# A recurrent attention block and a gated product: seven products for eight in the last six half blocks, with chunks placed every two steps and reordered sums

## The chip, the cores and the metric

The kernel runs on one core of a Trainium2 chip. Its engines work side by side, each through its own queue in order, and wait for each other by semaphores: PE multiplies matrices, DVE and POOL do elementwise work, ACT does activations and copies, SP issues most of the DMAs. Matmuls read SBUF and add up in PSUM[...]. The metric is the device time of one execution in microseconds (us), and the median over several runs is compared.

## The reference

All numbers are float32 on the chip (the two weight matrices of the second half come as float64 and are converted by the kernel).

```python
batch, n_heads, seq, head_dim = (4, 8, 768, 64)
gamma = 1.0 - 2.0 ** (-5.0 - np.arange(H))
for t in range(S):
    state = gamma[None, :, None, None] * state + np.einsum('bhd,bhe->bhde', k[:, :, t], v[:, :, t])
    y[:, :, t] = scale * np.einsum('bhd,bhde->bhe', q[:, :, t], state)

x = y.transpose(0, 2, 1, 3).reshape(B * S, H * D)      # 3072 x 512
h = x @ w_in                                           # 3072 x 2048
g = h - np.tanh(h)
out = g @ w_out                                        # 3072 x 512
```

## The kernel before

**Two halves that overlap.** The attention works in 24 chunks of 128 tokens (six to a batch). The second half works on 12 *half blocks* of 256 tokens (n = 0 to 11; a chunk is half of one), and within each on 8 tiles of 256 of the 2048 middle columns (m2 = 0 to 7). That makes 96 steps. The list `steps` (L492) has half blocks 0 to 3 first, in pieces of two or four tiles while the weights still arrive (32 steps), then half blocks 4 to 11 one after the other, eight tiles each (64 steps).

**One step** is an up product (`up`, L407: 8 matmuls of 256 columns into a bank h), an activation, and a down product (`down`, L456) of the tile two steps back (`LAG = 2`): for each of the two token halves j, two matmuls of 512 columns that add into a bank of output. The trace shows each float32 matmul of the program as two passes, so an up product has 16 passes and a down product 8.

**The activation** has five ACT instructions (`shrink_begin` L420, `shrink_factors` L427: a square, a tanh, two more squares and a relu), three DVE instructions (`shrink_multiply`, L436) and three more (`shrink_end`, L445), which leave g. The last tile of a run of tiles is followed by `add_up` (L465), which copies or adds the output bank into `sum` on DVE or ACT, and starts the store of the output on SP when the last weights are in it.

**A chunk of attention** is spread over three chunk steps. `load_chunk` (L222) loads k, q, v. `scale` (L232, on POOL) multiplies q and v by a power of gamma. `turn_by_dma` (L267) brings k and q into transposed form: two ACT copies split the words into 16-bit halves (`apart`, L273), SP stores them to DRAM (`rows`, L276) and reads them back through a transposing DMA into `kqT` (L278). `products` (L287) multiplies k with v (L298) and `kqT` with itself (L304, the scores); `mask` and `state` take the results off PSUM on DVE; `outputs` and `outputs_rest` (L336, L385) multiply into y (L352) with `see` (small ACT copies) between them; `keep_x` (L389) copies y into `xT`, the input of the up products.

**The order** is the program's own: nothing is moved by a scheduler. The first eight chunks and steps follow an order written out by hand (L547). From step 8 on the loop at L569 runs. `with_chunk` (L564) gives every third step a chunk ci: the step scales chunk ci+3, ends the outputs of ci, makes the products of ci+2, loads ci+4 and begins the outputs of ci+1. Its last act is to turn chunk ci+3. Steps 9 to 26 also convert one piece of weights each (four DVE instructions and two each on ACT and POOL) and load another on SP.

```python
with_chunk = {BEGUN + 3 * i + 1: FIRST - 3 + i for i in range(NCH - FIRST + 3)}
...
for s in range(BEGUN, len(steps)):
    ...
    shrink_begin(n, m2)
    shrink_factors(n, m2)
    shrink_multiply(n, m2)
    shrink_end(n, m2)
    downs(LAG)
    if ci is not None and ci + 3 < NCH:
        turn_by_dma(ci + 3)
```

PSUM is full: two banks for k and q products ("t"), two for y, two for h and two for the output sums ("o").

## The time and the profile before

| what | value |
|---|---|
| median of 9 runs | 754.64 us (754.43 to 755.52) |
| the profiled execution | 754.64 us, of which the span of the instructions is 752.8 us |
| granted clock of PE | 1.00 of full speed throughout |
| busy in 100 to 200 us: PE, DVE, ACT, POOL | 99.1, 91.6, 65.3, 48.6 us |
| busy in 350 to 450 us | 100.0, 61.4, 51.4, 8.2 us |
| busy in 550 to 650 us | 100.0, 59.9, 43.2, 0 us |
| DVE operation on 128x512, on 128x256 | 0.69 us, 0.42 us |
| POOL operation on 128x512 | 1.09 to 1.29 us |
| store of 256 KB of output, issue to landing | 2.0 us |

The span is the time from the first to the last instruction of one execution that the hardware profiler recorded. The three stretches are one with attention and weights still arriving, one with attention alone, and one with neither. An engine's queue is in order, so a wait of one instruction delays all behind it on that engine; but idle time of an engine that isn't the one that sets the end costs nothing.

### The profile page before, as it was taken

The page shows a single profiled execution, that of the slowest core. Times are in us where ns is not written, and L with a number is a line of the kernel's source. Part 1 is how long each engine was busy: PE and PEld are TensorE (multiplying, and loading weights), DVE is VectorE, ACT ScalarE, POOL GpSimd, SP SyncE. Part 2 cuts the span into 40 slices and gives each one's busy share as a digit, 9 for nine tenths or more (in the row PEclk, how much of TensorE's full clock was granted, in tenths as well). Part 3 has the DMA queues.
Part 4 walks back from the last instruction along what each step waited for, and adds up shares of the span by engine and source line. Part 5 has one row for each costly group of instructions (what it writes and reads, how often), then busy time and mean ns, then how long its engine had stood idle before and what let it go on. Part 6 is the DMA issues. An engine that isn't in the chain of part 4 may idle for free.

```text
span 752.8 us, 13801 instructions
## 1 busy us (share of the span) xinstructions
PE 740.1 (98%) x5470; PEld 502.4 (67%) x5470; DVE 519.4 (69%) x807; ACT 389.1 (52%) x725; POOL 126.6 (17%) x108
## 2 busy tenths in 40 slices
PE   8799999999999999999999999999999999999997
PEld 7686666666667676766676666666666666666663
DVE  4999889998898666656565656555665666556653
ACT  4567486667665545445545545444344434433441
POOL 0564445435453111100111100000000000000000
PEclk9999999999999999999999999999999999999999
DMA  9882436556553353332542412000000000000000
GB/s 204 210 213 59 127 99 179 148 151 157 151 128 90 92 137 118 85 85 76 107 99 73 97 57 58 28 1 1 29 0 1 28 1 0 29 0 1 28 2 28
DMA packets 125392, 59.76 MB, mean 79 GB/s; under 512 B 109840, under 2 KB 118160, under 8 KB 125328
## 3 DMA queue, kind: packets, MB, share of 16 engines
q1 hardware_dynamic: 125184, 58.73, 30.3%
q8 instruction: 43, 0.70, 0.4%
q10 hardware_dynamic: 144, 0.15, 0.1%
q14 instruction: 21, 0.17, 0.1%
HBM read 35.80 MB, written 14.68 MB: 67 GB/s over the span
## 4 chain that ended last, share of the span: by engine, by line
PE 87%; DVE 7%; DMA 2%; ACT 1%; issue 1%; SPq 1%; POOL 0%; DVEq 0%; ACTq 0%; POOLq 0%
PE h L414 40%; PE o L462 40%; PE y L352 3%; PE s L298 1%; PE s L304 1%; DVE head L185 1%; DMA raws<-in_moe_w_in_dram 1%; DVE h L448 1%; DVE g L452 1%; DVE head L183 1%; DVE h L442 1%; DMA q<-in_q_dram 1%; DMA k<-in_k_dram 1%; DVE th L439 1%; DVE g L453 1%
## 5 line engine op out<-in xcount | busy, mean ns | idle before, releaser
L414 PE MATMUL h<-xT,w 128*128 128x256 f32 x1536 | 349.9, 381 | 1.1 <-DVE w L199 1.1
L462 PE MATMUL o<-w,g 128*128 128x512 f32 x768 | 345.6, 593 | 1.4 <-DVE sum L471 0.9
L414 PEld LDWEIGHTS h<-xT,w 128*128 128x128 f32 x1536 | 289.7, 190 | 71.8 <-issue 34.0
L462 PEld LDWEIGHTS o<-w,g 128*128 128x128 f32 x768 | 145.4, 190 | 145.7 <-issue 136.6
L423 ACT ACTIVATE u<-h 128x512 f32<-128x512 f32 x96 | 57.4, 598 | 292.0 <-PE h L414 292.0
L439 DVE TENSOR_TENSOR th<-h,th 128x512 f32<-128x512 f32 x96 | 66.2, 690 | 176.0 <-ACT th L424 175.8
L453 DVE COPY_PREDICATED g<-large,th 128x512 f32<-128x512 int32 x96 | 72.2, 752 | 10.6 <-ACT apart L273 0.5
L442 DVE SCALAR_TENSOR_TENSOR h<-q,h 128x512 f32<-128x512 f32 x96 | 66.8, 696 | 10.4 <-DVE h L440 0.5
L448 DVE SCALAR_TENSOR_TENSOR h<-q,h 128x512 f32<-128x512 f32 x96 | 66.8, 696 | 9.9
L431 ACT ACTIVATE q<-u,tab 128x512 f32<-128x512 f32 x96 | 69.4, 723 | 0.0
L432 ACT ACTIVATE q<-u,tab 128x512 f32<-128x512 f32 x96 | 69.0, 719 | 0.0
L433 ACT ACTIVATE large<-u,tab 128x512 f32<-128x512 f32 x96 | 68.7, 716 | 0.0
L452 DVE TENSOR_TENSOR g<-h,u 128x512 f32<-128x512 f32 x96 | 66.3, 691 | 3.3
L440 DVE SCALAR_TENSOR_TENSOR h<-u,h 128x512 f32<-128x512 f32 x96 | 65.8, 685 | 0.0
L236 POOL TENSOR_TENSOR q<-q,tab 128x512 f32<-128x512 f32 x22 | 24.1, 1093 | 199.4 <-DMA q<-in_q_dram 158.1
L424 ACT ACTIVATE th<-h 128x512 f32<-128x512 f32 x96 | 56.8, 591 | 0.0
L195 POOL TENSOR_TENSOR low<-low,power 128x512 f32<-128x512 f32 x30 | 38.7, 1289 | 102.3 <-DVE power L187 78.1
L199 POOL TENSOR_TENSOR w<-low,head 128x512 f32<-128x512 f32 x30 | 38.5, 1282 | 2.4
L352 PEld LDWEIGHTS y<-a,v 64*64 64x64 f32 x768 | 15.8, 134 | 16.2 <-ACT large L433 10.6
L236 POOL TENSOR_TENSOR v<-v,tab 128x512 f32<-128x512 f32 x22 | 26.5, 1204 | 0.0
L382 ACT COPY seen<-y 64x1 f32<-64x1 f32 x96 | 10.1, 153 | 24.7 <-PE y L352 24.3
L393 ACT COPY xT<-y 128x512 f32<-128x512 f32 x24 | 14.1, 587 | 16.4 <-PE y L352 16.4
(49 smaller groups left out, 382.9 us busy)
## 6 DMA issues: line engine op xcount, KB each, us to landing
rows<-apart SPq DMA_DIRECT2D x16, 512.0 KB, 2.6
k<-in_k_dram SPq DMA_DIRECT2D x24, 256.0 KB, 4.0
q<-in_q_dram SPq DMA_DIRECT2D x24, 256.0 KB, 4.9
v<-in_v_dram SPq DMA_DIRECT2D x24, 256.0 KB, 5.3
raw<-in_moe_w_out_dram SPq DMA_DIRECT2D x12, 512.0 KB, 3.5
out_dram<-sum SPq DMA_DIRECT2D x24, 256.0 KB, 2.0
raw<-in_moe_w_in_dram SPq DMA_DIRECT2D x14, 256.0 KB, 4.1
raw<-in_moe_w_in_dram SPq DMA_DIRECT2D x28, 128.0 KB, 3.8
```

The lines of the kernel that those rows point to most:

```text
L414: nc.tensor.matmul(hp, w1[:, c, ts(2 * m2 + i, P)], xT[n // 2][:, c, ts(n % 2, TH)], start=(i == 0 and c == 0), stop=(c == NC - 1), skip_g ...
L423: nc.scalar.activation(u, hp, AF.Square)
L431: nc.scalar.activation(q0, u, AF.Square, bias=bias0)
L432: nc.scalar.activation(q1, u, AF.Square, bias=bias1, scale=math.sqrt(A))
L433: nc.scalar.activation(large, u, AF.Relu, bias=bias_m)
L439: nc.vector.tensor_tensor(th, hp, th, op=ALU.subtract)
L440: nc.vector.scalar_tensor_tensor(hp, in0=u, scalar=R, in1=hp, op0=ALU.subtract, op1=ALU.mult, reverse0=True)
L442: nc.vector.scalar_tensor_tensor(hp, in0=q0, scalar=C0, in1=hp, op0=ALU.add, op1=ALU.mult)
L448: nc.vector.scalar_tensor_tensor(hp, in0=q1, scalar=A * C1, in1=hp, op0=ALU.add, op1=ALU.mult)
L452: nc.vector.tensor_tensor(flat, hp, u, op=ALU.mult)
L453: nc.vector.copy_predicated(flat, large.bitcast(I32), th)
L462: nc.tensor.matmul(o_p[j], gT[n, m2][:, i, ts(j, P)], w2[:, 2 * m2 + i], start=(first and i == 0), stop=(last and i == 1))
```

## The change

The last six half blocks (n = 6 to 11) compute the down product by Winograd's form of Strassen's scheme. The 256 tokens are split into two sets of 128, the 256 middle columns into two of 128, and the 512 output columns into two of 256. Eight products of blocks become seven, with sums of blocks before and after:

- `fast_sums` makes four sums of blocks of g on POOL, 128x128 each, in each of the 48 steps.
- `fast_weights` makes four differences of blocks of the weights for each pair of tiles, 16 operations on POOL in all, one in each of the steps 33 to 48, in buffers that the weights' conversion and one `xT` no longer need.
- `fast_down` issues the seven matmuls, 256 columns wide, into halves of the banks that the attention and the sums held.
- `fast_end` recombines the seven results once for a half block: one ACT copy, seven DVE operations of 256 columns and two stores.

So that those banks are free, the chunks come every two steps rather than three and are over after step 45 (before: step 63). The outputs of the last chunk come behind the up product of their step. `downs` comes ahead of `shrink_end`. The tokens of a half block are dealt out alternately to its two sets, which makes `keep_x` two copies and the rows of each output store alternate.

```diff
@@ keep_x
-        nc.scalar.copy(
-            out=xT[n][:, :, ts(nj, P)].rearrange("p (n r) t -> p r n t", r=2),
-            in_=y_banks[:, ci % 2][:, :: 1 - 2 * (ci % 2)],
-        )
+        half = xT[n][:, :, ts(nj // 2, TH)].rearrange("p (n r) t -> p r n t", r=2)
+        y = y_banks[:, ci % 2][:, :: 1 - 2 * (ci % 2)]
+        for odd in range(2):
+            nc.scalar.copy(out=half[:, :, :, ds(P * odd + D * (nj % 2), D)],
+                           in_=y[:, :, :, odd::2])
@@ add_up
-            nc.sync.dma_start(out=out[ds(n * TH + j * P, P)], in_=o)
+            nc.sync.dma_start(out=rows_of(n)[:, j], in_=o)
...
+    FAST = 6
+    PAIRS = NM // 2
+    def quarter(i, c, at):
+        return w2[:, i::2, ts(c, TH)][:, ds(2 * at, 2)]
+    def fast_weights(k, at):
...
+        t = t_of[k, at] = room[PAIRS // 2 * k + at]
+        a, b = (
+            (quarter(0, 1, at), quarter(0, 0, at)),
+            (quarter(1, 1, at), t_of.get((0, at))),
+            (quarter(1, 1, at), quarter(0, 1, at)),
+            (t_of.get((1, at)), quarter(1, 0, at)),
+        )[k]
+        nc.gpsimd.tensor_tensor(t, a, b, op=ALU.subtract)
+    def fast_sums(n, m2):
+        g = gT[n, m2]
+        a11, a12, a21, a22 = (g[:, i, ts(j, P)] for j in range(2) for i in range(2))
+        s_ = inp.tile([P, 4, P], F32, tag="kq"[m2 % 2], name=f"s_{n}_{m2}", bufs=2)
+        s1, s2, s3, s4 = (s_[:, i] for i in range(4))
+        nc.gpsimd.tensor_tensor(s1, a21, a22, op=ALU.add)
+        nc.gpsimd.tensor_tensor(s2, s1, a11, op=ALU.subtract)
+        nc.gpsimd.tensor_tensor(s3, a11, a21, op=ALU.subtract)
+        nc.gpsimd.tensor_tensor(s4, a12, s2, op=ALU.subtract)
+        fast_g[n, m2] = (a11, a12, s4, a22, s1, s2, s3)
...
+    def fast_down(n, m2, first, last):
+        if first:
+            fast_banks(n)
+        left = fast_g.pop((n, m2))
+        for k in (1, 6, 5, 7, 4, 2, 3):
+            right = (
+                w2[:, 2 * m2, :TH], w2[:, 2 * m2 + 1, :TH], w2[:, 2 * m2 + 1, TH:],
+                *(t_of[x, m2 // 2][:, m2 % 2] for x in (3, 0, 1, 2)),
+            )[k - 1]
+            nc.tensor.matmul(accs[n][k], left[k - 1], right, start=first and k in (1, 6, 5, 4),
+                             stop=last, skip_group_check=True)
+    def fast_end(n):
+        acc = accs.pop(n)
+        o = op.tile([P, 2, DM], F32, tag="sum", name=f"sum_{n}")
+        c11, c12, c21, c22 = (o[:, j, ts(c, TH)] for j in range(2) for c in range(2))
+        some = [mid.tile([P, 2, TH], F32, tag="a", name=f"fast_{n}") for _ in range(2)]
+        p1, v_, x_, w_ = (t[:, i] for t in some for i in range(2))
+        nc.scalar.copy(out=p1, in_=acc[1])
+        for dst, k, b, how in (
+            (v_, 6, p1, add), (x_, 5, v_, add), (w_, 7, v_, add), (c22, 5, w_, add),
+            (c21, 4, w_, sub), (c11, 2, p1, add), (c12, 3, x_, add),
+        ):
...
@@ downs
+            if tile_[0] >= FAST:
+                fast_down(*tile_)
+                if tile_[3]:
+                    fast_end(tile_[0])
+                continue
@@ the loop
-    with_chunk = {BEGUN + 3 * i + 1: FIRST - 3 + i for i in range(NCH - FIRST + 3)}
+    with_chunk = {BEGUN + 2 * i + 1: FIRST - 3 + i for i in range(NCH - FIRST + 3)}
+    with_fast = {4 * NM // 2 + 1 + i: (i % 4, i // 4) for i in range(2 * PAIRS)}
...
-            if FIRST <= ci + 1 < NCH:
+            if FIRST <= ci + 1 < NCH - 1:
                 outputs(ci + 1)
                 see(ci + 1)
...
         for i in range(2):
             up(n, m2, i)
+        if ci == NCH - 2:
+            outputs(ci + 1)
+            see(ci + 1)
         waiting.append(steps[s])
         shrink_begin(n, m2)
         shrink_factors(n, m2)
         shrink_multiply(n, m2)
+        downs(LAG)
         shrink_end(n, m2)
-        downs(LAG)
+        if n >= FAST:
+            fast_sums(n, m2)
+        if s in with_fast:
+            fast_weights(*with_fast[s])
         if ci is not None and ci + 3 < NCH:
             turn_by_dma(ci + 3)
-    for j in range(2):
-        for tile_ in waiting:
-            part(j, *tile_)
+    downs(0)
```

The lines move by some numbers: what is L298 and L304 before is L302 and L308 after, `up` is L420, the new matmuls are L579.

## The prediction

> **What bounds the kernel now.** I read the busy times first, then the chain of waits, the chain's pieces late in the run, one whole chunk period on three engines, the DMA issues and the tail.

> ```profile
> span 752.8 us, 13801 instructions
> ...
> PE 740.1 (98%) x5470; PEld 502.4 (67%) x5470; DVE 519.4 (69%) x807; ACT 389.1 (52%) x725; POOL 126.6 (17%) x108
> ...
> PE 87%; DVE 7%; DMA 2%; ACT 1%; issue 1%; SPq 1%; POOL 0%; DVEq 0%; ACTq 0%; POOLq 0%
> ...
> 596.87 3.45 PE h L414 x16
> 600.33 3.43 PE o L462 x8
> ```

> PE works almost always and carries the chain: what leaves PE's queue shortens the run, what makes PE wait lengthens it. The last two lines are one step: an up product of 16 passes of 256 columns (3.45/16 = 0.2155 us each) and a down product of 8 passes of 512 columns (3.43/8 = 0.429). A step is 6.89 us.

> The second thing to read is one chunk period (timeline of PE, ACT and SP, times from the span's start).

> ```profile
> 330.74 0.46 PE L352 MATMUL y<-a,v 64*64 64x64 f32 x16
> 331.02 0.65 PE L298 MATMUL s<-v,k 64*64 64x64 f32 x32
> 331.49 0.65 PE L304 MATMUL s<-kqT 64*64 64x64 f32 x32
> 332.77 3.72 PE L414 MATMUL h<-xT,w 128*128 128x256 f32 x16
> 336.53 0.60 ACT L423 ACTIVATE u<-h 128x512 f32<-128x512 f32 x1 [3.17 <-PE h L414]
> 339.34 1.04 ACT L273 COPY apart<-k 128x1024 uint16<-128x1024 uint16 x1
> 340.27 1.05 ACT L273 COPY apart<-q 128x1024 uint16<-128x1024 uint16 x1
> 341.34 0.36 SPq L276 DMA_DIRECT2D rows<-apart  x1
> 344.03 1.86 SPq L278 DMA_TRANSPOSE kqT<-rows  x1
> 353.63 0.46 PE L352 MATMUL y<-a,v 64*64 64x64 f32 x16
> 354.38 0.65 PE L304 MATMUL s<-kqT 64*64 64x64 f32 x32
> ...
> kqT<-rows SPq DMA_TRANSPOSE x16, 4.2
> ```

> Call 330.74 the chunk's start. The transposed k and q of the next chunk come out of a fixed chain: up product, five activations, two copies to `apart` (over at +10.6), a store of `rows` that lands 2.7 later, and a transposing DMA that lands 4.1 to 4.2 after its issue, at +17.4. L304 of the next chunk needs them. It comes at 354.38, +23.6, so the chain has 6.2 us to spare and PE never shows a wait on it.

> The tail:

> ```profile
> 743.71 5.42 PE L462 MATMUL o<-w,g 128*128 128x512 f32 x12 [0.51 <-DVE g L453]
> 749.17 0.69 DVE L473 COPY sum<-o 128x512 f32<-128x512 f32 x1 [5.51 <-PE o L462]
> ```

> [...] the transpose is issued 2.69 us after `rows`, as soon as that has landed (2.6). Two such DMAs in series can't be pipelined within a chunk. [...] Here a load takes 190 ns against 215 ns of a 256-column pass, so halving the width stays just clear of the load. [...]

> **The change part by part.**

> *Seven products for eight.* For half blocks 6 to 11 (48 of 96 steps) a down product of 8 passes of 512 becomes 7 products of 256 columns, two passes each: 14 x 0.2155 = 3.02 us for 3.43. The loads have the up product's shape, which keeps 0.2155. Gain 0.42 x 48 = 20.2 us. If each pass lost 5 ns to loads it would be 16.8; below 0.2155 nothing points.

> *POOL's sums.* Four 128x128 operations per step stand between g and the product. POOL's 512-wide ones take 1.09 to 1.29; [...] a quarter of a row's time is 0.32, a full row's 1.29 bounds it. I take 0.4, 1.6 for four. A g is ready 5.6 us after its up product (600.33 to 605.94), its down product starts 12.9 after, so 7.3 is spare; with 2.9 of recombination before `shrink_end`, 4.4. Hidden, even nearly at the upper bound; only the last step shows it, about 0.2. The 16 weight differences (1.2 to 1.3 each, steps 33 to 48) lie in POOL's idle time.

> *Recombination.* Seven DVE operations of 256 columns (0.42, from the `state` rows) and an ACT copy per half block, before `shrink_end`. DVE has 40% idle there (59.86 busy of 100 in 550 to 650). Hidden five times, exposed once: the program lets the first of the seven wait for the last product of the bank it reads, so for the last half block all seven (3.05 us) follow the last matmul, against 0.69 now. From the end of the last up product (738.07) the span now lasts 14.7. After: three down products 9.05, stalls 0.3, 3.05, and 2.94 for the store as now, 15.3. So the end is 0.6 worse though three of the 48 savings (1.26) fall into it: 1.9 is taken off the 20.2.

> *Sums ahead of the last operations.* DVE's sums come out before L448. It removes the 0.86 us wait of PE for a sum at 144.5, and puts stores of out ahead of `rows` on SP. g gets 1.2 later where 7 are spare.

> *Last chunk's outputs behind an up product.* Removes a 0.70 us wait of PE for `xT` at 491.9.

> *x in two column halves.* Two ACT copies of 256 for one of 512: 0.2 longer, 24 times, beside ACT idle of 1 to 3 us before each square. I take 0.2 for the crowded opening, bounds 0 and 1.

> *Chunks every two steps instead of three.* `3 * i` becomes `2 * i`, so the attention's banks are free after step 45. The chunk period now is 353.63 - 330.74 = 22.89; with one step of 6.89 less it becomes 16.0 us. L304 then comes at 346.74 + 0.75 = 347.49 on the scale above, but the transposed operands land at 348.13 and reach PE about 0.1 later. PE waits 0.75 us. The delay doesn't fade: up, activations, copies and DMAs all start behind the wait, so each chunk pays anew. Nothing else in PE's in-order queue can fill it; outputs, up and down of the step queue behind. Sixteen chunks, 8 to 23, take this path:
> - Chunk 8: now the transpose is issued at 117.97 (SP waited behind weight loads, `rows` took 3.8) and lands 4.3 later; L304 would come a step before its 125.58, at 118.7. 3.6.
> - Chunk 9: two sums on ACT now come before its copies in the same step, 1.2; with the trace's 2.9 and 4.2, 2.6.
> - Chunk 10: 1.3 (its DMAs took 3.9 and 5.7 in the trace, which would give 3.6; the clean ones 0.95).
> - Chunks 11 to 16, weights still loading and loads of q, k, v denser: 0.75 plus 0.45, 7.2. In the trace such periods had excesses of 0 to 0.6.
> - Chunks 17 to 20: two stores of out stand in front of `rows`: 0.2 on SP and 0.4 to 0.7 in landing (3.06 at 297.98), 1.6 each, 6.4.
> - Chunks 21 to 23: 2.4 in all.
> - SP's long issues (a transpose of 3.56 us at 366.93 landed after 6.5): about 2.

> Sum 25.5. Bounds: with no excess beyond the clean chain 18.5; with every DMA as slow as the slower third, 34.

> *Total.* Gains 20.2 + 0.9 + 0.7 = 21.8; costs 25.5 + 1.9 + 0.2 = 27.6; net +5.8. The profiled execution took 754.64 (752.8 of span and 1.84 around it), which is also the median. 760.4.

> **The rivals.**
> - *The transposed operands come in time* (the other side). If they are usable some 0.8 us earlier than the landing times say, clean chunks don't wait, and about 10 us of stall remains (chunks 8 to 10, and little of 17 to 20): 754.6 - 21.8 + 12.1 = 745. It decides as soon as the mean wait per chunk is under 19.7/16 = 1.23 us. For it: the margin is only 0.75 in 17.4. Against: `rows` shows that the reported landing is when the next engine goes on.
> - *They cancel*: stalls at their lower bound 18.5, total 753.4.
> - *DVE or the DMAs become the bound while weights load.* Windows 100 to 200 have DVE 91.6% busy. Two steps then need 8.7 of activation, 4.0 of conversion, 1.4 of mask and state, 1.2 of sums, 15.3 of 16.8 us. If POOL's denser work slows conversions (L183 once took 1.38 for 0.43) by 2 us per period, or raw loads reach `rows` as at 158.5, nine chunks pay 1 to 1.5 more: 770.
> - *POOL's sums are late*: PE waits for POOL each fast step; at four times 1.29 only after recombinations, 6 x 1 us. Small, and held in the forecast's range.

> **How the numbers follow.** Forecast with stalls of 21.5 to 30: 0.55 (756 to 765). DVE or DMA bound: 0.15. Cancelling: 0.13. In time: 0.17. What this kernel's measurement can tell from no change is about 0.2%, 753.1 to 756.1. Faster: 0.17 and 0.03 of the cancelling, 0.20; same: its other 0.10 and 0.02 of the forecast, 0.12; slower 0.68. The range leaves a tenth on each side, into the middle of the fast case and of the slow one: 747 to 769.

> **What would show it.** PE should wait at L304 (now L308) for the `kqT` DMA about 16 times, 0.7 to 3.6 us each, all before about 400 us, and not after; a fast step should be 6.46 us; PE should finish with seven DVE operations behind it. No waits at L308, or a fast step near 6.9, would overturn the sum.

## The result and the profile after

The changed kernel takes 757.59 us (median of 9 runs, 757.06 to 759.05) against 754.64: ratio 1.0041, 95% interval 1.0032 to 1.0049. It is slower by 3 us, on the side that was forecast; the forecast was 5.8 slower (760.4). The profiled execution took 759.0, of which 756.9 is span; the one before had a span of 752.8.

The page of the kernel after, the same lines as before, and its group for the scores (`kqT` with itself, now L308; the last column is idle time of PE just before it and what ended it):

```profile
span 756.9 us, 14749 instructions
...
PE 727.3 (96%) x5758; PEld 561.2 (74%) x5758; DVE 534.5 (71%) x843; ACT 389.4 (51%) x749; POOL 231.4 (31%) x316
...
PE 70%; DMA 15%; DVE 6%; ACT 5%; issue 2%; SPq 0%; POOL 0%; DVEq 0%; ACTq 0%; POOLq 0%
...
L308 PE MATMUL s<-kqT 64*64 64x64 f32 x768 | 16.8, 226 | 16.8 <-DMA kqT<-rows 16.8
```

PE's busy time has fallen by 12.8 us, and the span has grown by 4.1. PE had 87% of the chain of waits and has 70%; DMAs have gone from 2% to 15%. That is a wait that wasn't there: PE stands still for 16.8 us in front of L308.

One chunk period of the kernel after (timeline of its engines; start, duration, engine, line; brackets are idle time before the instruction and what ended it):

```profile
328.25 0.65 PE L302 MATMUL s<-v,k 64*64 64x64 f32 x32
329.94 0.69 PE L308 MATMUL s<-kqT 64*64 64x64 f32 x32 [1.04 <-DMA kqT<-rows]
331.26 3.72 PE L420 MATMUL h<-xT,w 128*128 128x256 f32 x16
338.76 1.05 ACT L277 COPY apart<-q 128x1024 uint16<-128x1024 uint16 x1
339.84 0.36 SPq L280 DMA_DIRECT2D rows<-apart  x1
342.53 1.85 SPq L282 DMA_TRANSPOSE kqT<-rows  x1
345.51 0.65 PE L302 MATMUL s<-v,k 64*64 64x64 f32 x32
346.89 0.69 PE L308 MATMUL s<-kqT 64*64 64x64 f32 x32 [0.73 <-DMA kqT<-rows]
```

The two products of k and v are done, and L308 waits for the transposing DMA issued at 342.53. The chain from the up product (331.26) to its landing is about as long as before; with what stands ahead of it, it is longer than two steps. Each of the 16 chunks on this path waits: 3.66, 2.11 and 0.61 us in chunks 8 to 10, 0.53 to 0.79 in 11 to 16, 1.04 to 1.36 in 17 to 20 and 0.60 to 0.73 in 21 to 23.

A fast step, in PE's timeline:

```profile
562.94 3.62 PE L420 MATMUL h<-xT,w 128*128 128x256 f32 x16
566.39 0.59 PE L579 MATMUL fast_t<-w,g 128*128 128x256 f32 x2
...
569.41 1.46 PE L420 MATMUL h<-xT,w 128*128 128x256 f32 x6
```

From one up product to the next it is 569.41 - 562.94 = 6.47, where it was 6.89: 0.41 less, 48 times, 19.8 us.

What the prediction had not looked for stands behind the two longest waits. PE's timeline, then windows of 3.41 us around them (start and end, length, busy time of PE, PEld, DVE, ACT and POOL with counts, granted clock of PE, DMA share, GB/s):

```profile
122.29 1.13 PE L308 MATMUL s<-kqT 64*64 64x64 f32 x32 [3.66 <-DMA kqT<-rows]
123.35 4.86 PE L420 MATMUL h<-xT,w 128*128 128x256 f32 x16
...
141.27 0.69 PE L308 MATMUL s<-kqT 64*64 64x64 f32 x32 [2.11 <-DMA kqT<-rows]
...
142.59 5.41 PE L420 MATMUL h<-xT,w 128*128 128x256 f32 x16
```

```profile
118.88:122.29 3.41, 0.00 (x0) 0.00 (x1) 3.17 (x6) 0.00 (x0) 3.17 (x3) 1.00 0.83 184
122.29:125.70 3.41, 3.41 (x38) 2.84 (x39) 3.02 (x7) 0.00 (x0) 1.84 (x2) 0.50 1.04 233
125.70:129.11 3.41, 3.41 (x15) 2.64 (x14) 1.18 (x3) 0.86 (x2) 1.94 (x2) 1.00 1.11 220
139.36:142.77 3.41, 1.50 (x81) 1.44 (x82) 2.51 (x5) 0.04 (x1) 2.78 (x3) 1.00 1.02 256
142.77:146.18 3.41, 3.41 (x9) 2.70 (x10) 2.67 (x6) 1.62 (x6) 0.07 (x1) 0.50 1.22 224
```

The same up product that takes 3.72 takes 4.86 and 5.41: the granted clock is 0.50 for 3.41 us from 122.29 and again from 142.77 (as means of the 4 us from 122 and from 142, 0.57 and 0.60). With the slower L308 that is 1.6 and 1.7 us, 3.3 in sum, on top of the waits.

### The profile page after: what moved, and what is told of

Same layout as the page of the kernel before. It is cut to its first block, busy times and chain, and to the rows that moved or that the text cites. A ratio compares the mean times of both kernels' runs of the same rounds, so it can differ in the third digit from the quotient of the medians.

```text
span 756.9 us, 14749 instructions
## 1 busy us (share of the span) xinstructions
PE 727.3 (96%) x5758; PEld 561.2 (74%) x5758; DVE 534.5 (71%) x843; ACT 389.4 (51%) x749; POOL 231.4 (31%) x316
## 4 chain that ended last, share of the span: by engine, by line
PE 70%; DMA 15%; DVE 6%; ACT 5%; issue 2%; SPq 0%; POOL 0%; DVEq 0%; ACTq 0%; POOLq 0%
PE h L420 36%; PE o L468 10%; DMA kqT<-rows 8%; PE fast_t L579 7%; PE y L579 6%; PE fast_o L579 5%; DMA rows<-apart 5%; ACT apart L277 3%; PE y L356 2%; PE s L308 2%; PE kqTp L216 1%; DMA q<-in_q_dram 1%; ACT q L437 1%; ACT q L438 1%; PE kqTp L254 1%
## 5 line engine op out<-in xcount | busy, mean ns | idle before, releaser
L420 PE MATMUL h<-xT,w 128*128 128x256 f32 x1536 | 352.7, 383 | 1.1 <-DVE w L203 1.1
L420 PEld LDWEIGHTS h<-xT,w 128*128 128x128 f32 x1536 | 291.7, 191 | 53.5 <-issue 12.9
L468 PE MATMUL o<-w,g 128*128 128x512 f32 x384 | 173.0, 593 | 0.0
L468 PEld LDWEIGHTS o<-w,g 128*128 128x128 f32 x384 | 72.6, 190 | 71.4 <-issue 68.2
L544 POOL TENSOR_TENSOR s<-g 128x128 f32<-128x128 f32 x48 | 21.8, 455 | 294.6 <-DVE g L459 214.3
L459 DVE COPY_PREDICATED g<-large,th 128x512 f32<-128x512 int32 x96 | 74.1, 772 | 9.5
L448 DVE SCALAR_TENSOR_TENSOR h<-q,h 128x512 f32<-128x512 f32 x96 | 66.8, 696 | 10.8 <-DVE h L446 0.9
L308 PE MATMUL s<-kqT 64*64 64x64 f32 x768 | 16.8, 226 | 16.8 <-DMA kqT<-rows 16.8
L579 PE MATMUL fast_t<-w,g 128*128 128x256 f32 x96 | 28.6, 380 | 0.0
```

Source lines behind the costliest of these rows:

```text
L420: nc.tensor.matmul(hp, w1[:, c, ts(2 * m2 + i, P)], xT[n // 2][:, c, ts(n % 2, TH)], start=(i == 0 and c == 0), stop=(c == NC - 1), skip_g ...
L448: nc.vector.scalar_tensor_tensor(hp, in0=q0, scalar=C0, in1=hp, op0=ALU.add, op1=ALU.mult)
L459: nc.vector.copy_predicated(flat, large.bitcast(I32), th)
L468: nc.tensor.matmul(o_p[j], gT[n, m2][:, i, ts(j, P)], w2[:, 2 * m2 + i], start=(first and i == 0), stop=(last and i == 1))
L579: nc.tensor.matmul(accs[n][k], left[k - 1], right, start=first and k in (1, 6, 5, 4), stop=last, skip_group_check=True)
```

## The experiments

The theory: the seven products save about 20 us, the operands that come too late for the shorter chunk period cost somewhat more, and long waits lower PE's clock. The rivals: the waits at L308 are harmless, or come from somewhere else; the seven products have hidden costs; the clock falls for another reason. The kernel before was measured again beside each group of runs (755.64, 754.74, 754.67 and 754.78), so kernels of different groups are compared by their ratios to it.

| kernel | median us | ratio to before, 95% interval |
|---|---|---|
| before, chunks every two steps | 797.17 | 1.0543, 1.0526 to 1.0561 |
| after, operands turned early | 742.08 | 0.9820, 0.9803 to 0.9838 |
| after, waits of chunks 8 and 9 filled | 759.65 | 1.0047, 1.0029 to 1.0064 |
| after, chunks by three, four fast half blocks | 742.86 | 0.9834, 0.9820 to 0.9849 |
| after, sums last again | 785.95 | 1.0413, 1.0390 to 1.0436 |
| operands early, no fast half blocks | 758.92 | 1.0055, 1.0035 to 1.0076 |
| operands early, chunk 8 a step earlier | 738.09 | 0.9780, 0.9766 to 0.9793 |
| the same, accumulators in other banks | 737.09 | 0.9766, 0.9753 to 0.9780 |
| sums last, six long waits filled | 783.59 | 1.0384, 1.0360 to 1.0408 |
| the banks' kernel, outputs in front again | 737.97 | 0.9780, 0.9755 to 0.9805 |
| sums last, six waits filled to size | 776.29 | 1.0284, 1.0268 to 1.0300 |
| before, sums first | 753.57 | 0.9983, 0.9976 to 0.9989 |

**Is it the late operands?** Three runs. First, the rhythm alone, in the kernel before:

```diff
-    with_chunk = {BEGUN + 3 * i + 1: FIRST - 3 + i for i in range(NCH - FIRST + 3)}
+    with_chunk = {BEGUN + 2 * i + 1: FIRST - 3 + i for i in range(NCH - FIRST + 3)}
```

> The kernel before with the chunks every two steps and nothing else. If the transposed operands that come late are the cost: L304 waits for kqT in all 16 chunks, and the four chunks with output stores wait some 2 us longer than in the changed kernel, because the sums still come after the activation's last operations. 24 us of stalls in the changed kernel plus 4 x 2.2: about 785 us (778 to 790). If the denser chunks cost little and the seven products simply don't pay: 755.

797.17 us: the rival is out, but the cost is 41 us rather than 30. PE's waits (line waited at, cause: us in total, times, longest):

```profile
PE s L304 <- DMA kqT<-rows: 29.7, 16, 5.2
```

That is 13 us more than in the kernel after, nearly all of it in chunks 17 to 20, where it waits 5.20, 3.33, 4.31 and 3.78 for 1.36, 1.08, 1.11 and 1.04. Something else in the change holds these waits down; a later part finds it. Most of what the 41 us hold beyond the waits is lowered clock, which the sum had not counted for these chunks: from L304 to the next down product, chunks 17 to 20 took 7.76, 6.49, 7.44 and 6.46 us instead of 4.88 (4.65 in chunk 19), and chunk 8 took 5.87 instead of the 4.18 that it takes once its wait is filled, 10.6 in sum.

Second, the kernel after with the chain started sooner. The copies to `apart` stand right behind the up product, ahead of the five activations:

```diff
         for i in range(2):
             up(n, m2, i)
...
+        if ci is not None and ci + 3 < NCH:
+            turn_by_dma(ci + 3)
         waiting.append(steps[s])
         shrink_begin(n, m2)
...
-        if ci is not None and ci + 3 < NCH:
-            turn_by_dma(ci + 3)
```

> The changed kernel with the turn of chunk ci+3 put ahead of the step's activation, so that the two ACT copies come some 5 us sooner. Late operands: no waits at L308, no stretches of lowered clock, 757.6 - 24 = about 734 us. If what costs is the density of the attention work (DVE, DMA contention) and not the place of the copies: 745 or more.

742.08 us, ratio 0.982: faster than both kernels. Its timeline for the chunk that was at 331 in the kernel after:

```profile
313.44 0.65 PE L308 MATMUL s<-kqT 64*64 64x64 f32 x32
316.33 1.04 ACT L277 COPY apart<-q 128x1024 uint16<-128x1024 uint16 x1
317.40 0.86 SPq L280 DMA_DIRECT2D rows<-apart  x1
321.64 1.89 SPq L282 DMA_TRANSPOSE kqT<-rows  x1
```

L308 has no bracket, and the copies are over 317.37 - 313.44 = 3.9 us after it instead of 339.81 - 329.94 = 9.9. Of the 16 waits one is left, chunk 8's, still 3.4 us, since its copies and its store stood behind POOL's scaling and the weight loads on SP. That wait is part of why 734 was too low: the sum had taken away the stalls of all chunks, and chunk 8's cost 3.8 in the kernel after. Its span is 737.9 (739.99 us at clock 0.998), and the other three executions took 741.98 to 742.55 at 0.996, which a lowered clock behind that one wait could explain; they left no trace, so that is not shown.

Third, the kernel after with the old rhythm, which allows only four fast half blocks:

```diff
-    FAST = 6
+    FAST = 8
-    with_chunk = {BEGUN + 2 * i + 1: FIRST - 3 + i for i in range(NCH - FIRST + 3)}
+    with_chunk = {BEGUN + 3 * i + 1: FIRST - 3 + i for i in range(NCH - FIRST + 3)}
```

> The changed kernel with the chunks every three steps as before, and the seven products for half blocks 8 to 11 alone (32 steps), whose banks are free by then. Late operands: no waits at L308; 754.6 - 32 x 0.413 (13.2) - 1.6 for the two waits removed + 2.2 for the end = about 742 us. If the fast part costs something of its own that the sum misses: 750 or more.

742.86 us, as forecast, and no wait at L308 at all. So two half blocks more, bought with the faster rhythm, had cost more than three times what they bring: 16 steps at 0.41 are 6.6 us, the late operands some 23 (worked out below).

**What are the seven products worth by themselves?** The kernel with operands turned early, with eight products everywhere:

```diff
-    FAST = 6
+    FAST = 12
...
-        if s in with_fast:
+        if FAST < 2 * NB and s in with_fast:
```

> The changed kernel with the operands turned early, and with eight products in the last six half blocks too. The seven products saved 0.413 us in each of 48 steps, 19.8, less 2.0 for the longer tail: the time should be 17.8 above the run with the operands turned early, 759.9 us (758 to 762). Rival: the seven products bring less where nothing else waits, because POOL's sums, the recombination and the weight differences have a hidden cost: below 756 us.

1.0055 - 0.9820 = 0.0235 of 754.7 is 17.7 us (medians alone, from different groups, differ by 16.8). POOL's sums and the recombination show no cost beyond the tail; the two intervals leave about 2 us either way.

**What holds the waits of chunks 17 to 20 down?** The sums' place, undone in the kernel after:

```diff
-        downs(LAG)
-        shrink_end(n, m2)
+        shrink_end(n, m2)
+        downs(LAG)
```

> The changed kernel with one part undone: the down products, and with them the sums of a half block, stand again behind the activation's last operations. If the sums' place decides when the stores of out let the store of rows through on SP, the waits for kqT of chunks 17 to 20 grow from 1.1 to 1.4 us to 3.3 to 5.2 us as in the run of the chunks alone, some 12 us, and three or four clock drops of about 1.7 us come with them: about 776 us (768 to 782). Rival, as the prediction had it: the place is worth only the 0.86 us wait for a sum: about 758.5 us, and the waits of chunks 17 to 20 stay below 1.6.

785.95 us, 28 more than the kernel after, and beyond the range of either side. Timeline of chunk 18's chain in this run:

```profile
293.07 1.05 ACT L277 COPY apart<-q 128x1024 uint16<-128x1024 uint16 x1
294.17 0.75 DVE L459 COPY_PREDICATED g<-large,th 128x512 f32<-128x512 int32 x1
294.81 1.28 DVE L477 TENSOR_TENSOR sum<-o,sum 128x512 f32<-128x512 f32 x2
295.52 0.95 SPq L484 DMA_DIRECT2D out_dram<-sum  x2
296.56 0.41 SPq L280 DMA_DIRECT2D rows<-apart  x1
299.61 1.88 SPq L282 DMA_TRANSPOSE kqT<-rows  x1
...
303.83 0.69 PE L308 MATMUL s<-kqT 64*64 64x64 f32 x32 [3.36 <-DMA kqT<-rows]
```

and in the kernel after:

```profile
286.47 1.28 DVE L477 TENSOR_TENSOR sum<-o,sum 128x512 f32<-128x512 f32 x2
287.10 1.05 ACT L277 COPY apart<-q 128x1024 uint16<-128x1024 uint16 x1
287.18 0.95 SPq L484 DMA_DIRECT2D out_dram<-sum  x2
288.23 0.41 SPq L280 DMA_DIRECT2D rows<-apart  x1
```

SP's queue is in order, as these lines show. With the sums last, SP stands at the first store of out until DVE has done the sum, and `rows`, whose data was ready at 294.12, goes out at 296.56, 2.4 late. With the sums first, the stores have left when the copies end at 288.15, and `rows` follows 0.1 later. In all four chunks `rows` goes out 2.4 late, and in chunk 17 it then took 5.35 to land where it took 3.05 in the kernel after. Of the 28: waits at L308 in chunks 17 to 20 are 16.65 in sum instead of 4.59, 12.1 more; the lowered clock behind them costs 9.0 (the last section has the stretches); and the recombination, now also late, makes PE wait 4.5 for sums of L597 (2.6 and 1.9 in its list of waits). The remaining 2.5 were not taken apart.

The same edit in the kernel before, where chunks come every three steps:

```diff
-        shrink_end(n, m2)
-        downs(LAG)
+        downs(LAG)
+        shrink_end(n, m2)
```

> The kernel before with one part of the change alone: the down products, and with them the sums of a half block, ahead of the activation's last operations; chunks stay every three steps. If this place is worth what the prediction took, the wait of 0.86 us for a sum goes and 753.8 us remain (753 to 754.6, with before at 754.7). Rival: here too the stores of out hold up the transposed operands, and the gain is over 3 us.

753.57 against 754.78, 1.2 us. One edit is thus worth 1.2 us in one rhythm and 28 in the other: there 6 us of slack lay under `rows`, here none.

**Does waiting itself lower the clock?** Matmuls on constants, whose result is never used, were put into PE's queue between L302 and L308 of the chunks that wait long. First 13 for chunk 8 and 7 for chunk 9 in the kernel after:

```diff
+        for _ in range({8: 13, 9: 7}.get(ci, 0)):
+            nc.tensor.matmul(sp[:, 0, :P], busy, busy, start=True, stop=True,
+                             skip_group_check=True)
```

> The changed kernel with matmuls of zeros between L302 and L308 in chunks 8 and 9 alone (13 and 7), which fill the two longest waits. In the changed kernel the up products behind these waits took 4.86 and 5.41 us in place of 3.67, with the granted clock at 0.57 and 0.60. If idleness of PE lowers the clock: both take 3.7 again, and 2 to 3.5 us are gained, about 755. If the clock falls for another reason (the burst of DMAs): unchanged, 757.6.

759.65: no gain. But PE's timeline shows that the fills did what they were made for, and why the time didn't follow:

```profile
118.72 3.17 PE L305 MATMUL s<-busy 128*128 128x128 f32 x26
122.58 0.69 PE L311 MATMUL s<-kqT 64*64 64x64 f32 x32 [0.70 <-DMA kqT<-rows]
123.21 3.72 PE L423 MATMUL h<-xT,w 128*128 128x256 f32 x16
...
260.59 1.13 PE L311 MATMUL s<-kqT 64*64 64x64 f32 x32 [2.71 <-DMA kqT<-rows]
...
262.93 4.22 PE L423 MATMUL h<-xT,w 128*128 128x256 f32 x16
```

Both up products behind the fills take 3.72, and chunk 10's scores come at 156.59 instead of 159.79. Then, in chunk 16, one store of `rows` took 4.57 us from issue to landing where 2.7 is usual; the wait became 2.71 and the clock fell there. Whether the other executions lost their gain in the same way is not known: they have no trace.

So the question was put to a kernel with more at stake: the one with the sums last, with its six long waits filled. The first try took a fill matmul for 0.12 us. In the profile it is two passes (20 matmuls took 4.73 us in chunk 18), so the fills of chunks 17 to 20 lasted 7.2 us longer in sum than the waits that they were to fill:

```diff
+        for _ in range({8: 13, 9: 7, 17: 36, 18: 20, 19: 26, 20: 20}.get(ci, 0)):
```

> The run with the sums last again, with 13, 7, 36, 20, 26 and 20 matmuls on constants (128 columns each, some 0.12 us) in PE's queue between L302 and L308 of chunks 8, 9, 17, 18, 19 and 20, where PE waits 2 to 5.7 us for kqT. They compute nothing that is used, and end about when the operands come. If idleness of PE lowers its clock, the stretches from L308 to the end of the next up product lose the 2.9, 1.6, 2.6 and 1.6 us that they took over 4.9 in chunks 17 to 20, and the 1.7 of chunk 8: 775.5 us (772 to 779) against 785.95, with granted clock near 1.00. Rival: the clock there falls for another reason, such as the traffic of the DMAs, and the fills change nothing: 783 or more.

783.59, hardly less than 785.95, with no lowered clock left before the tail. With the sizes put right:

```diff
+        for _ in range({8: 13, 9: 7, 17: 20, 18: 11, 19: 15, 20: 12}.get(ci, 0)):
```

> As the run with long waits filled, but with 13, 7, 20, 11, 15 and 12 matmuls for chunks 8, 9, 17, 18, 19 and 20: one of them takes 0.236 us, not 0.12, so that the fills of chunks 17 to 20 ended 7 us too late in sum. Now they end before the operands come. If the lowered clock is PE's idleness, the time comes to 775.5 us (773 to 779), the same waits and all up products at 3.6 to 3.7 us. Rival: other waits take the gain back, as with chunks 8 and 9 filled: 782 or more.

776.29: 1.0413 - 1.0284 = 0.0129, or 9.7 us, come back for work that is thrown away. The group of the up products, with the sums last and then with the fills to size (busy time in us and mean ns of a pass):

```profile
L420 PE MATMUL h<-xT,w 128*128 128x256 f32 x1536 | 358.0, 387 | 1.1 <-DVE w L203 1.1
```

```profile
L423 PE MATMUL h<-xT,w 128*128 128x256 f32 x1536 | 349.9, 381 | 1.1 <-DVE w L203 1.1
```

349.9 is what the same 1536 passes took in the kernel before. The DMAs run as they did: over chunks 17 to 20 they moved 116 GB/s with the sums last (270 to 350 us, mean granted clock 0.89) and 122 GB/s with the fills (268.7 to 346.7 us, clock 1.00). So the rival is out: PE's idleness lowered its clock.

**Better versions.** Chunk 8's last wait, by starting that chunk a step earlier:

```diff
+    with_chunk[BEGUN] = with_chunk.pop(BEGUN + 1)
```

> The changed kernel with the operands turned early, and the loads, scaling and turning of chunk 8 a step earlier still. The one wait left there is 3.4 us for chunk 8's kqT at 122 us. If it goes, and with it the lowered clock that followed it in some executions, 737 us (735.5 to 739) against 742.08. Rival: chunk 8's store and transposition are held by the weight loads on SP wherever they stand: the wait stays above 2 us and the time at 741 to 743.

738.09. Chunk 8's wait is gone, and chunk 9 now waits 1.67 us, behind which the clock did not fall. On top of it, the seven accumulators in banks by the order in which they are finished:

```diff
-        acc = {1: first, 2: first, 5: second, 7: second, 3: third, 4: third, 6: sixth}
-        right = {2: 1, 7: 1, 4: 1, 6: n % 2}
+        acc = {1: first, 6: first, 5: second, 7: second, 4: third, 2: third, 3: sixth}
+        right = {6: 1, 7: 1, 2: 1, 3: n % 2}
...
-            nc.tensor.matmul(accs[n][k], left[k - 1], right, start=first and k in (1, 6, 5, 4),
+            nc.tensor.matmul(accs[n][k], left[k - 1], right, start=first and k in (1, 5, 4, 3),
```

> As the run before it, and the seven accumulators paired in banks in the order in which they are finished (1 with 6, 5 with 7, 4 with 2, 3 in the bank of its own) instead of 1 with 2, 5 with 7, 3 with 4 and 6 alone. If the seven sums of the last half block all come after the last matmul because the first of them waits for product 2's bank, they now start some 2 us before it and only one or two follow it: 1.7 us less than the run before it (1.2 to 2.2), 735.3 us. Rival: the sums wait for the whole group of banks that hold one allocation, and nothing changes: the same time within 0.5 us, seven sums behind the last matmul.

737.09 us, 1.0 less than the run before it rather than 1.7. The tail of the kernel after, then of this one:

```profile
750.52 0.59 PE L579 MATMUL y<-w,s 128*128 128x256 f32 x2
750.72 0.37 ACT L588 COPY fast<-fast_t 128x256 f32<-128x256 f32 x1 [6.38 <-PE fast_t L579]
751.22 0.42 DVE L597 TENSOR_TENSOR fast<-y,fast 128x256 f32<-128x256 f32 x1 [4.15 <-PE y L579]
...
753.47 0.41 DVE L597 TENSOR_TENSOR sum<-y,fast 128x256 f32<-128x256 f32 x1
```

```profile
728.12 0.59 PE L579 MATMUL fast_t<-fast_power,s 128*128 128x256 f32 x2
...
728.76 0.37 ACT L588 COPY fast<-fast_t 128x256 f32<-128x256 f32 x1 [5.51 <-PE fast_t L579]
...
729.16 1.21 DVE L597 TENSOR_TENSOR fast<-fast_t,fast 128x256 f32<-128x256 f32 x3 [3.19 <-ACT fast L588]
...
729.42 0.59 PE L579 MATMUL y<-w,s 128*128 128x256 f32 x2
```

The first copy now starts before the last matmul has started, but still waits for product 7 (728.12), which lies in the other bank of the same two-bank buffer `fast_t`. That would account for the missing 0.7 us; no run gave these products buffers of their own. This is the fastest kernel of the study: 2.3% under the kernel before.

In it, last, the outputs of chunk 23 put in front of the up product again:

```diff
-            if FIRST <= ci + 1 < NCH - 1:
+            if FIRST <= ci + 1 < NCH:
...
-        if ci == NCH - 2:
-            outputs(ci + 1)
-            see(ci + 1)
```

> The run with accumulators paired by their end, with the last chunk's outputs ahead of the up product again, as they stood before. If that place saves what the prediction took, PE waits 0.7 us for xT once more: 737.8 us (737.4 to 738.3) against 737.09. Rival: the outputs' 24 passes fill another wait there, or the xT is in time now: within 0.3 us of 737.09, with no wait for xT after 300 us.

737.97, with executions from 736.36 to 740.50 and an interval that covers the run without the edit: the time settles nothing. The trace shows the wait for `xT` once more, 0.8 us, where the prediction took 0.7.

## Why the prediction was right, and where it wasn't

The sum was: gains 21.8, costs 27.6, net +5.8. Measured in the two profiled spans: gains 19.8 + 0.86 + 0.70 = 21.4, costs 22.8 of chunks and 2.0 of the tail (0.8, and three of the 48 savings that lie in it), net +3.4, with +4.1 seen and 0.7 not assigned. The median is 1.4 under the profiled execution of 759.0: the executions with a mean granted clock of 0.993 or 0.994 took 758.2 to 759.05 us, those with 0.995 to 0.997 took 757.06 to 757.59.

- *Seven for eight*: 20.2 forecast, 19.8 in the trace, and 17.7 with the tail's cost in a run of its own (17.8 from the same terms). Right: weight loads don't show in the step, since 30 passes of 0.2155 make 6.47, with PEld busy for 87.9 of the 100 us from 500 to 600 (66.7 before); the 0.4 are a slip, since the prediction's 3.43 - 3.02 is 0.41 and not 0.42.
- *Late operands, no filling, paid anew by each chunk*: right in mechanism and count, 16 waits and none after 400 us. The sizes of 25.5 were off in both directions. The waits listed are 16.8: chunks 11 to 16 wait 0.63 on average instead of 1.2, chunks 17 to 20 1.15 instead of 1.6, chunk 10 0.6 instead of 1.3, chunk 9 2.1 instead of 2.6. The 2 us for long issues on SP did not come: no transpose took SP over 2.4 us.
- *What the chunks lose beyond the listed waits*: L308 goes from 346.89 to 363.72 to 380.67, 0.77 and 0.89 over the 16.06 that the same periods take with the operands turned early, where 0.60 and 0.69 are listed. Without a wait L308 starts 0.47 after L302, whose end is put at 0.65, and a listed wait counts from that end; so each hides 0.18, 2.9 in sum. From chunk 8's L308 to chunk 23's it is 258.4 us, against 239.4 with the operands turned early, where chunks 9 to 23 don't wait: a loss of 19.0, and about 3.8 in chunk 8. That the sum, 22.8, is close to the forecast is in part luck: it holds 3.3 of lowered clock that the prediction hadn't thought of. Without them the chunks of this execution would cost 19.5, just under the 19.7 (1.23 for each of 16) at which the prediction saw the side decided, and of the 4.1 us between the spans 0.8 would be left. So the wait was foreseen for the right reason, but that it made the kernel clearly slower hung on a cost that was not foreseen.
- *Sums ahead of the last operations*: the step that failed. It was priced by what the trace of before showed, a wait of 0.86, and its stores were taken for a burden on `rows`. In the old rhythm 1.2 is measured; in the new one the place is worth 28 us, because the stores that it moves forward would otherwise hold `rows` up by 2.4 us in four chunks, and the longer waits bring lowered clock. The forecast wasn't hurt, as it priced the stores as they stand in the change. The chunks alone, forecast at 785, took 797 because the waits of these four chunks were longer by 3.0 us each and not by the 2.2 that the expectation allowed, and because 8.9 of lowered clock came with them.
- *POOL's sums*: hidden, 0.4 in the last step (0.2 forecast). A 128x128 operation takes 0.455 us, where the author's estimate was 0.4.
- *The tail*: 15.5 us from the end of the last up product, 15.3 forecast, with all seven DVE operations behind the last matmul, as said.
- *Last chunk's outputs*: the wait of 0.70 is gone.
- *The rivals*: in time (745) fell with the first wait of the list. DVE or the DMAs as the bound (770) fell too: chunks 11 to 16, in the crowded stretch, wait least. Cancelling (753.4) asked for 18.5 us of stall, 4.3 less than there were.

## What to carry to other kernels

When a stage is shortened, lay the longest chain that runs beside it, with its DMAs, against the new period before counting the saving; here 17.4 us against 16.0, and starting the chain behind the up product instead of behind its activation turned a loss of 0.4% into a gain of 1.8%. Price each part of a change in the schedule that the other parts make: an edit worth 1.2 us alone carried 28. And on an in-order queue of DMAs, as SP's is here (`rows` left 2.4 us late behind the stores of out), put a transfer that waits for late data behind the one that somebody is waiting for. The run with operands turned early does so, among other things: its `rows` goes out ahead of the step's stores of out, and chunks 17 to 20 don't wait.

## What the runs showed of the hardware

In these runs a long wait of PE mostly cost more than its length. In the traces without fills, and behind chunk 16 of the first filled run, there are 17 waits of 2 us or more at the scores. Behind 14 of them (2.11, 2.71 and 3.33 to 5.69 us) the next up product took 4.22 to 5.98 us instead of 3.62 to 3.72; behind three (2.06, 2.10 and 3.40 us) it didn't. Behind waits of 1.67 us and less at the scores it never did. In the kernel with the sums last, the stretch from L308 to the next down product took 7.78, 6.49, 7.50 and 6.50 us in chunks 17 to 20 for 4.88 normally (4.65 in chunk 19), 9.0 in sum.

```profile
117.12:120.53 3.41, 1.70 (x35) 0.75 (x33) 3.20 (x8) 2.68 (x4) 1.27 (x1) 1.00 0.36 81
120.53:123.94 3.41, 1.72 (x37) 1.55 (x38) 3.17 (x5) 1.05 (x1) 3.36 (x3) 1.00 0.99 238
123.94:127.35 3.41, 3.41 (x16) 2.62 (x15) 2.73 (x7) 0.74 (x2) 0.79 (x2) 1.00 1.28 225
```

Each keeps half of its time busy, and the clock stays. So it is in all traces between 100 us and the tail: every window in which PE was busy for 1.54 us or less was followed by one at half clock, and at full clock no window with 1.70 or more was; between the two there is no case. A window at half clock was followed by a second one when PE was busy for 66 to 81% of it, and by full clock when PE was busy for 99% or more. From 1.54 and 1.70 an estimate, for these kernels: a wait under some 1.7 us (3.41 - 1.70), half a window, doesn't lower the clock alone, and a longer one does it or not by where it falls. A wait of 1.87 us for a sum at 568 us did, in the last filled run (busy 1.54 of 3.41). Where the windows begin differs from run to run: one starts at 122.29 in the kernel after and at 123.69 with the sums last, though the waits of chunk 8 end within 0.2 us of each other.

What one lowered window costs a PE that is busy throughout can be estimated from the same records: half of 3.41 us, 1.7, and the up product of chunk 9 in the kernel after lost that (5.41 - 3.72). In these kernels waits of 1.87, 2.11 and 2.71 us, each shorter than a window, were enough for it, with PE busy for up to 1.54 us of the window before.
